# First transform of an SSM's response: data stationary against a moving constant, or the constant stationary against moving data

## The chip, the core and the metric

The kernel runs on one core of one Trainium2 chip. The metric is the device time of one execution in microseconds (us); less is better. A core has five engines that run side by side, each through its own instruction stream in order: TensorE (PE, with its weight loads shown apart as PEld), VectorE (DVE), ScalarE (ACT), GpSimd (POOL) and SyncE (SP). Matmuls write to PSUM, of which a tile of 128 x 512 floats is one bank; the other engines empty it. SP and POOL issue nearly all of this kernel's DMAs.

## The reference

The output is a sum of three parts over `x` of 2048 positions and 576 channels, normalised to `xn`:

```python
x = A_u
xn = _layernorm(x, axis=-1)
return x + _A_ref(xn, ...) + _B_ref(xn, B_w1, B_w2)

# _A_ref: a state space model as a long convolution, 128 complex states for each channel
P = jnp.exp(logdA[:, :, None] * l[None, None, :])
K = jnp.einsum("dn,dnl,dn->dl", Cc, P, dB).real          # response, 576 x 2048
...
y = irfft2(rfft2(xn padded) * rfft2(K padded)) + xn * Dskip
# _B_ref
out = silu(xn @ w1) @ w2                                   # 576 -> 4608 -> 576
```

## The kernel before

**Two streams.** The feed-forward part (`ffn()`, the "main" stream) is a chain of matmuls: `ph` (L298 to L300) makes 128 hidden rows for 512 positions, ScalarE and VectorE turn them into `gh` and `gl` (L306 to L308), and `po` (L328) multiplies these with `w2` and is added to `acc` by VectorE (L333). The convolution and all else are the "side" stream. A function `weave` interleaves the two by a table of fractions (`marks`), so that the side work is written in between. The order in which the instructions then stand on each engine is not that of the code: the framework's scheduler plays the program through with its own estimates of time and lets each engine take what is ready first, with `high_priority` and `issue_after` (`behind`) as hints. This order is fixed when the program is built. At run time each engine goes through its list, and an instruction that waits holds up all behind it on that engine.

**Rounded parts.** Matmuls of plain float32 show as two records each in the profile. The kernel therefore splits most operands into a rounded high part and the rest (`F32R`; names ending in h and l) and multiplies high x high, high x low and low x high, one fast record each. L298 and L328 are such; the two matmuls that the change touches, `kp` and `z`, were plain float32.

**The response.** `kgen` walks through 36 chunks of 16 channels. For a chunk VectorE and ScalarE make angles (`th`, L809, L811, L826), sines and cosines (L825 to L829), magnitudes (`mag`, in the tile `C`, L830 and L834) and from these two tables `S` and `C` (L845, L846). The magnitudes are products of powers: `powers` (L792 to L805), called for two chunks at a time, holds in `pw` the powers 0 to 7 of four bases per channel. It copies the bases in on ScalarE (L795) and makes the rest with three VectorE products (L800: square; L801: powers 3 and 4; L802: powers 5 to 7), and then `al` (L804). `S` and `C` have two buffers each.

After every second chunk, 18 times in all, TensorE contracts the tables over the 128 states into one PSUM bank `kp`: 64 matmuls of 32 x 64 (L866), K for 32 channels as 32 x 64 matrices of time. I call this event "a kp", and what lies between two of them "a stretch". ScalarE copies `kp` to `kt` (L873). Then comes the first transform `z` (L881), the subject of the change: for each of four column groups and two halves of the partitions, a 64 x 128 piece of `kt` is loaded as the stationary operand and the constant `f1` (64 x 128) moves. The two halves of the array work on different data at once (`tile_position` 0 and 64) and fill one PSUM bank each. ScalarE copies the two banks to `stage` (L889), and after every fourth chunk SP stores `stage` to `d1k` in DRAM (L894).

**The input's first transform.** `spread` is woven into `kgen`, one step per chunk from the third chunk on: `xn` is split (L149, L150), multiplied with the constant `s1` (L154, L155; `s1` holds both rounded parts of the same 128 x 128 constant, 128 stationary columns), copied to `u1` (L156) and stored by POOL to `d1u` (L157). `u1` has one buffer.

**After the response** the second half of the hidden layer goes on by Winograd's scheme, whose operands (`s1l`, `s2l`, ...) VectorE and ScalarE prepare in `wino_x` (L596 to L635) as soon as `kgen` is written; then `spectral` reads `d1u` and `d1k` back and does the second transforms, and `conv` the last. PSUM's pool `pss` has three banks, which `kp`, the two `z`, and `spread`'s `pu` share.

Of the kernel before, what the change touches and what calls it, by code (L numbers as in the profile page):

```python
# [10 lines left out]
F32 = mybir.dt.float32  # L11
# [30 lines left out]
def kernel(  # L42
# [14 lines left out]
    cs1: bass.AP,  # L57
    cf1: bass.AP,
    cm23: bass.AP,
# [28 lines left out]
    ident = cst.tile([P, P], F32, name="ident")  # L88
    f1 = cst.tile([P, P], F32, name="f1")
    s4 = None  # L90
# [47 lines left out]
    def spread(up):  # L138

        s1 = up.tile([P, 2, P], F32R, name="s1", bufs=1)  # L140
        nc.gpsimd.dma_start(s1, cs1)
        for j in range(NJ):
            src = up.tile([P, D], F32, tag="xr", name="xr")
            nc.sync.dma_start(src, dxn[:, j])
            for m in range(2):
                lo, hi = slice(64 * m, 64 * m + 64), slice(64 - 64 * m, 128 - 64 * m)
                u1 = up.tile([P, D], F32, tag="u1", name="u1")
                sp = up.tile([P, D], F32R, tag="sp", name="sp")
                nc.scalar.copy(sp[lo, :], src[lo, :])  # L149
                nc.vector.tensor_sub(sp[hi, :], src[lo, :], sp[lo, :])  # L150
                for h in range(2):
                    hs = slice(h * HD, (h + 1) * HD)
                    pu = pss.tile([P, 512], F32, tag="pss", name="pu")
                    nc.tensor.matmul(pu[:, :HD], s1[:, 0, :], sp[:, hs], start=True, stop=False)  # L154
                    nc.tensor.matmul(pu[:, :HD], s1[:, 1, :], sp[:, hs], start=False, stop=True)  # L155
                    nc.scalar.copy(u1[:, hs], pu[:, :HD])  # L156
                nc.gpsimd.dma_start(  # L157
                    d1u.rearrange("(p m j) d -> m j p d", m=2, j=NJ)[m, j], u1)
                yield j
# [477 lines left out]

    kl = yp = pa = kfp = w1x = tail_at = None
    kf = {}

    def natural(nat):
# [47 lines left out]
        r = nat.tile([P, 4 * D], F32, tag="r", name="r")  # L689
        for k, lag in enumerate((256.0, 64.0, 8.0, 1.0)):  # L690
            nc.scalar.activation(ex.rearrange("n (d k) -> n k d", k=4)[:, k, :], lrT, AF.Tanh, scale=0.5 * lag)
# [65 lines left out]

    def kgen():
        fT, rhoT, phiT = (kf[n] for n in ("f", "rho", "phi"))
        with tc.tile_pool(name="kg", bufs=1) as kg, tc.tile_pool(name="stg", bufs=1) as stg:  # L760
# [31 lines left out]
            def powers(i):  # L792
# [7 lines left out]
                nc.vector.tensor_mul(pv[:, :, 2], pv[:, :, 1], pv[:, :, 1])  # L800
                nc.vector.tensor_mul(pv[:, :, 3:5], pv[:, :, 1:3], pv[:, :, 2:3].broadcast_to([P, R, 2]))  # L801
                nc.vector.tensor_mul(pv[:, :, 5:8], pv[:, :, 1:4], pv[:, :, 4:5].broadcast_to([P, R, 3]))  # L802
                for q in range(2):
                    nc.vector.tensor_mul(split(al[:, q]), split(pw[:, q, :, 1, 0:4]), col(rhoT, i + q, 4))  # L804
                return al  # L805
# [12 lines left out]
            for i in range(NCK):  # L818
# [16 lines left out]
                    mag[:, :, 32:96].rearrange("n d (x y) -> n d x y", y=8),  # L835
                    pk[:, :, 2, :].unsqueeze(3).broadcast_to([P, W, 8, 8]),
                    pk[:, :, 3, :].unsqueeze(2).broadcast_to([P, W, 8, 8]))
                if i + 1 < NCK:
# [16 lines left out]
                for e in (1, 0):  # L855
                    S, C = tabs[e]
                    for gl in range(2):
                        for gp_ in range(2):
                            o = e * 256 + (gl * 2 + gp_) * 64
                            for q in range(4):  # L860
                                ch = gp_ * CH + gl * 4 + q
                                dst = kp[32 * q:32 * q + 32, o:o + 64]
                                begins = e == 1 and gl == 0 and gp_ == 0
                                with tc.high_priority(), behind(None if begins else first):
                                    for n, t in enumerate((C, S)):
                                        mm = nc.tensor.matmul(dst, t[:, ch, :32], t[:, ch, 32:],  # L866
                                                              start=begins and n == 0, stop=True,
                                                              tile_position=(0, 32 * q), skip_group_check=True)
                                if begins:
                                    first = mm.ins  # L870
                tabs = []
                kt = kg.tile([P, 512], F32, tag="kt", name="kt")
                nc.scalar.copy(kt, kp)  # L873

                z = [pss.tile([P, 512], F32, tag="pss", name="z") for _ in range(2)]
                first = None
                for eg in range(4):
                    for h in (1, 0):
                        rows = slice(64 * h, 64 * h + 64)
                        with tc.high_priority(), behind(first):  # L880
                            mm = nc.tensor.matmul(z[h][:, eg * P:(eg + 1) * P], kt[rows, eg * P:(eg + 1) * P], f1[rows],  # L881
                                                  start=True, stop=True, tile_position=(64 * h, 0))
                        first = first or mm.ins
                r = (i - 1) % NRUN
                if r == 0:
                    stage = stg.tile([P, 64, NRUN * CH], F32, tag="stage", name="stage")
                sv = stage[:, :, r * CH:(r + 2) * CH].rearrange("p k (e h c) -> p h e k c", h=2, c=2)
                for h in range(2):
                    nc.scalar.copy(sv[:, h], z[h].rearrange("p (e k c) -> p e k c", e=4, c=2))  # L889
# [132 lines left out]
    def side():  # L1022
        nonlocal s4, kl, yp, pa, kfp, w1x, tail_at
        marks = (0.1357, 0.613, 0.855)
# [9 lines left out]
        with tc.tile_pool(name="kf", bufs=1) as kfp:  # L1034
            for n in ("f", "rho", "phi"):
                kf[n] = kfp.tile([P, D], F32, name=n + "T")
            with tc.tile_pool(name="nat", bufs=1) as nat, tc.tile_pool(name="pb", bufs=2) as pb:
                nt = natural(nat)
                tiles = iter(range(8, NJ, 2))
                for at, tables in ((0.0, 1), (0.02, 0), (0.035, 0), (gate_of(1), 1), (0.06, 0), (gate_of(2), 1), (0.08, 0), (0.085, 1)):  # L1040
# [7 lines left out]
            with behind(pins["sd"]):  # L1048
                nc.gpsimd.dma_start(f1, cf1)
            nc.sync.dma_start(vt, cv)  # L1050
            with tc.tile_pool(name="up", bufs=1) as up, tc.tile_pool(name="w1x", bufs=1) as w1x:
                sp = spread(up)
                for n, at in enumerate(kgen()):
                    if n > 1:
# [41 lines left out]
def _constants():  # L1096
# [4 lines left out]
    cs = np.stack([np.cos(th), np.sin(th)], 2)  # L1101
    s1 = np.zeros((2, 2, 32, 32, 2, 2), f8)
    f1 = np.zeros((2, 2, 32, 32, 2, 2), f8)
    for q in range(2):
        s1[:, q, :, :, :, q] = cs
        f1[:, q, :, :, :, q] = cs
    s4 = np.broadcast_to(cs.transpose(2, 1, 0) / L, (2, 2, 32, 32)).reshape(P, 32)
    s1 = np.stack(_hi_lo(s1.reshape(P, P)), 1)
    f1 = f1.reshape(P, P)
    n2 = np.arange(64)  # L1110
# [21 lines left out]
        "cs1": s1,  # L1132
        "cf1": f1,
        "cm23": m23,
# [27 lines left out]
```

## Time and profile before

| what | value |
|---|---|
| median of 3 runs | 1121.45 us (1119.86 to 1123.09) |
| the profiled execution | 1121.59 us, its span 1119.7 us |
| busy over the span: PE, DVE, ACT, POOL | 97%, 85%, 65%, 13% |
| granted TensorE clock | 1.0 throughout |
| the stage of the 18 kp | 170 to 658 us of the span |
| z (L881) | 288 records, that is 144 matmuls |
| stores to d1u | 32 of 288 KB from POOL |

The span is the time from the first to the last instruction that the profiler shows; the execution's own time has 1.9 us more around it. A row of a group of instructions gives its line, engine and operation, what it writes and reads, its shapes and count, then busy time and mean duration, then the idle time of its engine just before and what ended it. Matmuls overlap one another, so the duration of one record is longer than the step from one to the next, and the step is what counts; on VectorE and ScalarE too one instruction starts a little before the one ahead has ended.

### The profile page before, as it was taken

The numbers are of one execution on the slowest core, as the hardware profiler recorded it, in microseconds if no ns is written. First come the engines' busy times: TensorE is split into PE (matmuls) and PEld (weight loads), VectorE is DVE, ScalarE is ACT, GpSimd is POOL, SyncE is SP. The second block draws the span as 40 slices with busy tenths as digits, with TensorE's granted clock in tenths as the row PEclk, the third lists the DMA queues.
The fourth block names the chain that finished last, engine by engine and source line by source line (L and its number), as shares of the span: only waits on it lengthen the run. The fifth ranks groups of instructions, "written<-read, shape, count | busy, mean of one in ns | idle before, by whom it ended". The sixth has DMA issues, their size and how long they took to land.

```text
span 1119.7 us, 23109 instructions
## 1 busy us (share of the span) xinstructions
PE 1091.6 (97%) x9101; PEld 987.6 (88%) x9101; DVE 950.0 (85%) x1615; ACT 728.1 (65%) x1285; POOL 140.5 (13%) x244
## 2 busy tenths in 40 slices
PE   6998999999999999999999999999999999999998
PEld 5997989889988899898899988899989998999787
DVE  6698899999999999999999978988878888886333
ACT  4665455776777766676667645877767877785330
POOL 1022100000000000000330001112212112111220
PEclk9999999999999999999999999999999999999999
DMA  9455632436353536356964235456455565543985
GB/s 272 141 156 177 194 124 82 144 85 176 105 154 128 150 108 172 120 138 236 237 190 92 72 65 183 133 175 178 140 165 178 163 187 157 167 157 116 247 200 139
DMA packets 161870, 173.68 MB, mean 155 GB/s; under 512 B 88497, under 2 KB 127425, under 8 KB 161121
## 3 DMA queue, kind: packets, MB, share of 16 engines
q1 hardware_dynamic: 137200, 106.75, 34.5%
q0 software_dynamic: 23888, 63.67, 19.2%
q10 hardware_dynamic: 672, 1.77, 0.7%
q8 instruction: 72, 1.18, 0.4%
q14 instruction: 38, 0.30, 0.1%
HBM read 109.64 MB, written 62.60 MB: 154 GB/s over the span
## 4 chain that ended last, share of the span: by engine, by line
PE 70%; DVE 10%; DMA 9%; ACT 5%; issue 4%; SPq 1%; POOL 1%; ACTq 0%; DVEq 0%; POOLq 0%
PE po L328 30%; PE ph L298 16%; PE pb L453 5%; PE kp L866 3%; DMA w<-dw 2%; PE pc L453 2%; DMA w1r<-in_B_w_dram 2%; PE pb L994 2%; PE pu L994 2%; PE pk L994 2%; PE ph L299 1%; PE ph L300 1%; PE z L881 1%; PE pa L453 1%; DMA w2r<-in_B_w_dram 1%
## 5 line engine op out<-in xcount | busy, mean ns | idle before, releaser
L328 PE MATMUL po<-w,gh 128*128 128x288 f32 x2304 | 475.1, 297 | 6.2 <-ACT w L284 2.1
L328 PEld LDWEIGHTS po<-w,gh 128*128 128x128 f32 x2304 | 376.5, 188 | 22.1 <-DMA w<-dw 2.7
L328 PE MATMUL po<-w,gl 128*128 128x288 f32 x1152 | 334.9, 296 | 0.6 <-DVE gl L308 0.6
L328 PEld LDWEIGHTS po<-w,gl 128*128 128x128 f32 x1152 | 215.2, 188 | 2.6 <-DVE gl L308 0.9
L333 DVE TENSOR_TENSOR acc<-po,acc 128x288 f32<-128x288 f32 x296 | 130.3, 452 | 59.7 <-PE po L328 58.6
L298 PE MATMUL ph<-xh,w1h 128*128 128x512 f32 (+1 forms) x368 | 99.1, 388 | 0.9 <-ACT xh L123 0.7
L298 PE MATMUL ph<-xl,w1h 128*128 128x512 f32 (+1 forms) x368 | 98.5, 386 | 0.0
L298 PE MATMUL ph<-xh,w1l 128*128 128x512 f32 (+1 forms) x368 | 97.9, 383 | 0.0
L306 ACT ACTIVATE gf<-ph 128x512 f32<-128x512 f32 (+1 forms) x92 | 53.3, 579 | 60.4 <-PE ph L300 41.8
L298 PEld LDWEIGHTS ph<-xl,w1h 128*128 128x128 f32 x368 | 67.6, 191 | 12.8
L298 PEld LDWEIGHTS ph<-xh,w1l 128*128 128x128 f32 x368 | 66.6, 189 | 11.7
L298 PEld LDWEIGHTS ph<-xh,w1h 128*128 128x128 f32 x368 | 65.2, 191 | 11.2 <-ACT xh L123 1.0
L157 POOL DMA_DIRECT2D d1u<-u x32 | 17.5, 547 | 405.8 <-ACT u L156 404.5
L825 ACT ACTIVATE c<-th,magic 128x1040 f32<-128x1040 f32 x36 | 42.0, 1168 | 40.2 <-DVE C L846 28.0
L307 ACT CAST gh<-gf 128x512 fp32r<-128x512 f32 (+1 forms) x92 | 55.3, 602 | 15.5 <-PE po L328 14.5
L903 POOL DMA_DIRECT2D m<-in_cm_dram x64 | 33.9, 531 | 250.8 <-PE pu L994 147.1
L308 DVE TENSOR_TENSOR gl<-gf,gh 128x512 fp32r<-128x512 f32 (+1 forms) x92 | 60.7, 662 | 3.5 <-ACT gh L307 3.3
L827 ACT ACTIVATE c<-th 128x1040 f32<-128x1040 f32 x36 | 38.7, 1076 | 33.7 <-DVE th L826 33.6
L845 DVE TENSOR_TENSOR S<-th,C 128x1024 f32<-128x1024 f32 x36 | 44.0, 1222 | 12.1 <-ACT th L828 12.0
L470 DVE TENSOR_TENSOR gl<-gf,gh 128x512 fp32r<-128x512 f32 x56 | 38.0, 688 | 11.9 <-ACT gh L469 11.6
L370 ACT CAST w1h<-w1r 128x512 fp32r<-128x512 f32 (+2 forms) x56 | 34.6, 621 | 20.3 <-DMA w1r<-in_B_w_dram 14.6
L826 DVE SCALAR_TENSOR_TENSOR th<-c,th 128x1040 f32<-128x1040 f32 x36 | 44.5, 1237 | 0.7 <-ACT c L825 0.5
(271 smaller groups left out, 2384.5 us busy)
## 6 DMA issues: line engine op xcount, KB each, us to landing
w1r<-in_B_w_dram SPq DMA_DIRECT2D x35, 512.0 KB, 4.2
dw<-w SPq DMA_DIRECT2D x28, 576.0 KB, 4.5
w<-dw POOLq DMA_DIRECT2D x28, 576.0 KB, 6.6
w2r<-in_B_w_dram SPq DMA_DIRECT2D x44, 288.0 KB, 5.0
d1u<-u POOLq DMA_DIRECT2D x32, 288.0 KB, 2.7
d1k<-stage SPq DMA_DIRECT2D x18, 512.0 KB, 7.3
ur<-d1u SPq DMA_DIRECT2D x32, 288.0 KB, 3.3
kr<-d1k SPq DMA_DIRECT2D x32, 288.0 KB, 2.8
```

What stands on the lines that cost most here:

```text
L298: nc.tensor.matmul(ph, w[:, kt, :], v[:, kt, a:e], start=n + kt == 0, stop=False)
L306: nc.scalar.activation(gf, ph, AF.Silu)
L307: pins["gh"] = nc.scalar.copy(gh, gf).ins
L308: pins["gl"] = nc.vector.tensor_sub(gl, gf, gh).ins
L328: pins["pe"] = nc.tensor.matmul(po[:, :HD], gs[g][:, js], ws[:, w, hs], start=n == 0 and j not in begun, stop=n == 3 * len(terms) - 1, ski ...
L333: nc.vector.tensor_add(acc[j][:, hs], po[:, :HD], acc[j][:, hs])
L453: pins["pe"] = nc.tensor.matmul(dst, a[:, kt], v[:, kt], start=start and n == 0, stop=stop and n == 5, skip_group_check=True).ins
L825: nc.scalar.activation(c65, th, AF.Identity, bias=magic)
L826: nc.vector.scalar_tensor_tensor(th, c65, MAGIC, th, op0=ALU.subtract, op1=ALU.subtract)
L827: nc.scalar.activation(c65, th, AF.Abs)
L845: nc.vector.tensor_mul(ov3, t[:, :, 0:64].rearrange("n d (x y) -> n d x y", y=32), mv3)
L994: nc.tensor.matmul(dst, st, mv[:, hs], start=n == 0, stop=n == 3 * len(terms) - 1)
```

## The change

Four things change, all in `kgen`, `spread` and the constants.

- `z` is turned round. The constant is stationary (`s1`, both rounded parts, which `spread` uses too), and the data move, 512 columns at a time: `kp` is split into `kh` (ScalarE, in place of the copy `kt`) and `kl` (a new VectorE subtraction that reads PSUM), and for each half of the partitions there are three matmuls: high x high, low part of the constant x high, high part of the constant x `kl`. Six matmuls of 512 columns replace eight of 128 in plain float32. `kl` takes the buffer of `u1`, so that the two exclude each other.
- One constant serves both transforms. The constant `f1` and its tile go; the columns of `s1` are put in the order (q, k, c). For `spread` the rows of `u1` come out in that order, so its store is two DMAs of 64 partitions each. For `kgen` the channels in `kp` are placed differently, and the result has k over the partitions; the copy to `stage` now reads PSUM with a step of 64 floats, and the store to `d1k` sends 64 neighbouring rows from each partition. Each element of that store is still 32 floats long.
- Powers 2 and 4 are made by ScalarE (`Square`, on 128 and 96 elements per partition) behind its copy of the bases; VectorE keeps power 3 (128 elements) and powers 5 to 7 (288 elements in place of 384). The base that needs no powers above 3 moves to the last place.
- `s1` is loaded ahead of `kgen`.

```diff
     def spread(up):
 
-        s1 = up.tile([P, 2, P], F32R, name="s1", bufs=1)
-        nc.gpsimd.dma_start(s1, cs1)
+        du = d1u.rearrange("(k q m j) d -> m j q k d", q=2, m=2, j=NJ)
...
-                nc.gpsimd.dma_start(
-                    d1u.rearrange("(p m j) d -> m j p d", m=2, j=NJ)[m, j], u1)
+                for q in range(2):
+                    nc.gpsimd.dma_start(du[m, j, q], u1[64 * q:64 * q + 64])
...
-                pv = pw.rearrange("n r d k e -> n (r d k) e")
-                R = 2 * W * 4
-                nc.vector.tensor_mul(pv[:, :, 2], pv[:, :, 1], pv[:, :, 1])
-                nc.vector.tensor_mul(pv[:, :, 3:5], pv[:, :, 1:3], pv[:, :, 2:3].broadcast_to([P, R, 2]))
-                nc.vector.tensor_mul(pv[:, :, 5:8], pv[:, :, 1:4], pv[:, :, 4:5].broadcast_to([P, R, 3]))
+                pv = pw.rearrange("n r d k e -> n (r d) k e")
+                nc.scalar.activation(pv[:, :, :, 2], pv[:, :, :, 1], AF.Square)
+                nc.scalar.activation(pv[:, :, 0:3, 4], pv[:, :, 0:3, 2], AF.Square)
+                nc.vector.tensor_mul(pv[:, :, :, 3], pv[:, :, :, 1], pv[:, :, :, 2])
+                nc.vector.tensor_mul(pv[:, :, 0:3, 5:8], pv[:, :, 0:3, 1:4],
+                                     pv[:, :, 0:3, 4:5].broadcast_to([P, 2 * W, 3, 3]))
...
-                kt = kg.tile([P, 512], F32, tag="kt", name="kt")
-                nc.scalar.copy(kt, kp)
+                kh = kg.tile([P, 512], F32R, tag="kh", name="kh")
+                kl = up.tile([P, D], F32R, tag="u1", name="kl")[:, :512]
+                nc.scalar.copy(kh, kp)
+                nc.vector.tensor_sub(kl, kp, kh)
 
                 z = [pss.tile([P, 512], F32, tag="pss", name="z") for _ in range(2)]
                 first = None
-                for eg in range(4):
+                for n, (k, v) in enumerate(((0, kh), (1, kh), (0, kl))):
                     for h in (1, 0):
                         rows = slice(64 * h, 64 * h + 64)
                         with tc.high_priority(), behind(first):
-                            mm = nc.tensor.matmul(z[h][:, eg * P:(eg + 1) * P], kt[rows, eg * P:(eg + 1) * P], f1[rows],
-                                                  start=True, stop=True, tile_position=(64 * h, 0))
+                            mm = nc.tensor.matmul(z[h], s1[rows, k], v[rows], start=n == 0, stop=n == 2,
+                                                  tile_position=(64 * h, 0))
...
-                sv = stage[:, :, r * CH:(r + 2) * CH].rearrange("p k (e h c) -> p h e k c", h=2, c=2)
+                sv = stage[:, :, r * CH:(r + 2) * CH].rearrange("p n (e h c) -> p h e n c", h=2, c=4)
                 for h in range(2):
-                    nc.scalar.copy(sv[:, h], z[h].rearrange("p (e k c) -> p e k c", e=4, c=2))
+                    nc.scalar.copy(sv[:, h], z[h].rearrange("p (e c n) -> p e n c", e=2, c=4))
...
-                    kv = d1k.rearrange("(k n) (g d) -> g n k d", n=64, g=2)
+                    kv = d1k.rearrange("(k n) (g d) -> g k n d", n=64, g=2)
```

Since the scheduler plans the whole program anew, the order of all engines differs from the first kp on, also in instructions that the diff does not touch. The lines of the changed program are up to 3 lower than those before at the same place (L328 becomes L325, L298 L295). Three places show it.

TensorE behind the tenth kp, before: the eight matmuls of `z` stand in one block, ahead of `spread`'s `pu`.

```order
L328 MATMUL po<-w_4706,gh 128x288 x2
L328 MATMUL po<-w_4706,gl 128x288 x2
L328 MATMUL po<-w_4504,gh 128x288
L881 MATMUL z<-f_69,kt 128x128 x8
L154 MATMUL pu<-sp,s_2126 128x288
L155 MATMUL pu<-sp,s_2126 128x288
```

The same place now:

```order
L325 MATMUL po<-w_5274,gh 128x288 x2
L325 MATMUL po<-w_5274,gl 128x288
L880 MATMUL z<-kh,s_1388 128x512 x4
L325 MATMUL po<-w_5425,gh 128x288 x2
L880 MATMUL z<-kl,s_1388 128x512 x2
L151 MATMUL pu<-sp,s_1388 128x288
L152 MATMUL pu<-sp,s_1388 128x288
```

The four matmuls that need `kh` alone and the two that need `kl` are parted by others; so it is behind each of the 18 kp.

VectorE behind the tenth kp, before: the products of powers, spread among the tables.

```order
L800 TENSOR_TENSOR pw<-pw 128x128
L333 TENSOR_TENSOR acc_247<-po,acc_247 128x288
L845 TENSOR_TENSOR S<-th,C 128x16x2x32
L846 SCALAR_TENSOR_TENSOR S<-th,C 128x16x32
L801 TENSOR_TENSOR pw<-pw 128x128x2
L150 TENSOR_TENSOR sp<-xr,sp 64x576
L845 TENSOR_TENSOR C<-c_5309,C 128x16x2x32
L846 SCALAR_TENSOR_TENSOR C<-c_5309,C 128x16x32
L809 TENSOR_TENSOR th<-vt,fT 128x1040
L802 TENSOR_TENSOR pw<-pw 128x128x3
```

The same place now (L843 and L844 are the tables, L283 and L305 the rests `w2` and `gl` of the main stream):

```order
L872 TENSOR_TENSOR kl<-kp,kh 128x512
L330 TENSOR_TENSOR acc_293<-po,acc_293 128x288
L305 TENSOR_TENSOR gl<-gf,gh 128x512
L283 TENSOR_TENSOR w_5425<-w2r,w_5425 128x576
L305 TENSOR_TENSOR gl<-gf,gh 128x512
L843 TENSOR_TENSOR C<-c_5336,C 128x16x2x32
L283 TENSOR_TENSOR w_5431<-w2r,w_5431 128x576
L798 TENSOR_TENSOR pw<-pw 128x128
L844 SCALAR_TENSOR_TENSOR C<-c_5336,C 128x16x32
L807 TENSOR_TENSOR th<-vt,fT 128x1040
```

`kl` has come in and one product of powers is gone; and the main stream's `gl` and `w2` splits now crowd into this stretch, ahead of the tables that the eleventh kp waits for.

ScalarE behind the tenth kp, now:

```order
L792 COPY pw<-eb 128x128
L303 ACTIVATE gf<-ph 128x512
L796 ACTIVATE pw<-pw 128x128
L888 COPY stage<-z 128x2x64x4 x2
L304 CAST gh<-gf 128x512
L153 COPY u_4860<-pu 128x288
L797 ACTIVATE pw<-pw 128x32x3
```

Before, the copy of the bases stood there with no square behind it. The second square now stands behind the copies of `z` and `pu`, which wait for TensorE.

More of the change, by code (lines that the diff above doesn't have):

```diff
@@ L57 @@
     cs1: bass.AP,
-    cf1: bass.AP,
     cm23: bass.AP,
@@ L689, in natural @@
         r = nat.tile([P, 4 * D], F32, tag="r", name="r")
-        for k, lag in enumerate((256.0, 64.0, 8.0, 1.0)):
+        for k, lag in enumerate((256.0, 8.0, 1.0, 64.0)):
             nc.scalar.activation(ex.rearrange("n (d k) -> n k d", k=4)[:, k, :], lrT, AF.Tanh, scale=0.5 * lag)
@@ L856, in kgen @@
                     S, C = tabs[e]
[L857 to L870, printed above, removed]
+                    for c4 in range(4):
+                        o = e * 256 + c4 * 64
+                        for q in range(4):
+                            ch = q % 2 * CH + q // 2 * 4 + c4
+                            dst = kp[32 * q:32 * q + 32, o:o + 64]
+                            begins = e == 1 and c4 == 0
+                            with tc.high_priority(), behind(None if begins else first):
+                                for n, t in enumerate((C, S)):
+                                    mm = nc.tensor.matmul(dst, t[:, ch, :32], t[:, ch, 32:],
+                                                          start=begins and n == 0, stop=True,
+                                                          tile_position=(0, 32 * q), skip_group_check=True)
+                            if begins:
+                                first = mm.ins
@@ L1047, in side @@
                             phase0(pb, (j, j + 1))
-            with behind(pins["sd"]):
-                nc.gpsimd.dma_start(f1, cf1)
             nc.sync.dma_start(vt, cv)
             with tc.tile_pool(name="up", bufs=1) as up, tc.tile_pool(name="w1x", bufs=1) as w1x:
+                s1 = up.tile([P, 2, P], F32R, name="s1", bufs=1)
+                with behind(pins["sd"]):
+                    nc.gpsimd.dma_start(s1, cs1)
                 sp = spread(up)
-                for n, at in enumerate(kgen()):
+                for n, at in enumerate(kgen(up)):
                     if n > 1:
```

21 lines of the change are left out of this document (8 added, 13 removed).

## The prediction

> **What bounds the kernel now.** I read the page's shares of busy time first (the table ahead has them: TensorE leads), then the busy times by stretch, then the waits, then the timeline around one z.
>
> ```profile
> 170.00:651.00 481.00, 479.55 (x4980) 432.50 (x4979) 459.28 (x676) 330.25 (x492) 37.36 (x72) 1.00 0.50 139
> 650.00:700.00 50.00, 48.34 (x410) 42.69 (x409) 39.39 (x62) 26.77 (x48) 6.23 (x11) 1.00 0.52 138
> ```
>
> These are the stage of the kp and the 50 us behind it (columns: stretch, length, then busy PE, PEld, DVE, ACT, POOL). In the stage TensorE has no gap to speak of, but VectorE is busy for 459.3 of 481 us too: 95%. What each waits for there:
>
> ```profile
> PE po L328 <- DVE acc L333: 0.6, 1, 0.6
> PE po L328 <- ACT gh L307: 0.5, 1, 0.5
> ...
> DVE C L830 <- PE kp L866: 5.7, 7, 1.4
> ```
>
> TensorE waits 1.1 us in 481 (total, times, longest), so its work sets the pace, and VectorE follows by little. VectorE cannot run far ahead: with two buffers of `C` it waits for the kp that still reads one (L830). How far ahead it is shows in the end of the last table of a pair (its start and duration, VectorE's timeline) against the start of the kp that reads it (chain of waits, which is a few hundredths late):
>
> ```profile
> 473.83 0.68 DVE L846 SCALAR_TENSOR_TENSOR C<-c,C 128x512 f32<-128x512 f32 x1
> ```
>
> ```profile
> 476.52 1.99 PE kp L866 x124
> ```
>
> and, two kp later,
>
> ```profile
> 506.98 0.68 DVE L846 SCALAR_TENSOR_TENSOR C<-c,C 128x512 f32<-128x512 f32 x1
> ```
>
> ```profile
> 512.18 2.00 PE kp L866 x125
> ```
>
> These are the smallest lead of the 18, 2 us, and the largest, 4.5; I use 3.1.
>
> **The change part by part.** *z on TensorE.* Its timeline, in three cuts:
>
> ```profile
> 480.81 0.29 PE L328 MATMUL po<-w,gl 128*128 128x288 f32 x1
> 481.04 0.49 PE L881 MATMUL z<-f,kt 64*128 64x128 f32 x4
> 481.04 0.60 PE L881 MATMUL z<-f,kt 64*128 64x128 f32 x6
> 481.04 1.16 PE L881 MATMUL z<-f,kt 64*128 64x128 f32 x16
> 482.13 0.40 PE L154 MATMUL pu<-sp,s 128*128 128x288 f32 x1
> ```
>
> and a later place where halves of the array work side by side:
>
> ```profile
> 1044.80 0.39 PE L453 MATMUL pb<-s2h,w1l 128*128 128x512 f32 x1
> 1045.12 0.69 PE L1013 MATMUL py<-ys,s 64*32 64x288 f32 x8
> 1045.74 0.50 PE L453 MATMUL pb<-s2h,w1l 128*128 128x512 f32 x1
> ```
>
> ```profile
> 441.76 2.72 PE ph L298 x12
> 472.42 4.11 PE po L328 x31
> ```
>
> From the chain (last fence), a 512-column matmul of rounded parts steps 2.72/12 = 0.227 us and a 288-column one 4.11/31 = 0.133. The step into z is 481.04 - 480.81 = 0.23, 0.10 more than a po; from z's start to the next matmul it is 1.09. So z costs 1.19. Two more records lengthen it by 0.11 (0.49 to 0.60): the two halves run together, eight pairs make 0.88, and 0.31 is for going in, filling and coming out. At the py matmuls two steps of four records take 0.62, of which 2 x 0.11 x 288/128 = 0.50 is columns, and the way in 0.32 - 0.23 = 0.09: 0.21 for one block of long matmuls. The new z has three pairs of 512 columns in two blocks: 3 x 0.227 + 2 x 0.21 = 1.10, which I round up for the trace's step of 0.01 to 1.12. That is 0.07 less than 1.19, times 18: **-1.3 us**. Bounds: 0.31 for each block gives 1.30 and +2.0; 0.19 (way in and out only) gives 1.06 and -2.3. Split in two by `kl`, the change pays for its shorter z nearly all that it gains.
>
> That the halves overlap was shown for plain float32, which takes a column at half the rate. [...]
>
> *VectorE's work.* Its prices are the mean durations less the overlap with the next instruction:
>
> ```profile
> L333 DVE TENSOR_TENSOR acc<-po,acc 128x288 f32<-128x288 f32 x127 | 55.0, 452 | 3.2 <-PE po L328 2.9
> L308 DVE TENSOR_TENSOR gl<-gf,gh 128x512 fp32r<-128x512 f32 x64 | 43.8, 686 | 0.1
> L826 DVE SCALAR_TENSOR_TENSOR th<-c,th 128x1040 f32<-128x1040 f32 x34 | 42.1, 1237 | 0.6 <-ACT c L825 0.5
> L845 DVE TENSOR_TENSOR S<-th,C 128x1024 f32<-128x1024 f32 x34 | 41.5, 1222 | 11.2 <-ACT th L828 11.1
> L268 DVE TENSOR_TENSOR w1l<-w1r,w1h 128x640 fp32r<-128x640 f32 x32 | 25.2, 817 | 0.0
> L286 DVE TENSOR_TENSOR w<-w2r,w 128x576 fp32r<-128x576 f32 x32 | 24.1, 752 | 0.0
> L150 DVE TENSOR_TENSOR sp<-xr,sp 64x576 fp32r<-64x576 f32 x31 | 23.3, 753 | 1.0
> L801 DVE TENSOR_TENSOR pw<-pw 128x256 f32<-128x256 f32 x16 | 10.0, 626 | 0.1
> L802 DVE TENSOR_TENSOR pw<-pw 128x384 f32<-128x384 f32 x16 | 8.9, 555 | 0.1
> L800 DVE TENSOR_TENSOR pw<-pw 128x128 f32<-128x128 f32 x16 | 6.9, 432 | 0.0
> L804 DVE TENSOR_TENSOR al<-pw,rhoT 128x64 f32<-128x64 f32 x32 | 5.7, 221 | 0.0
> ```
>
> ```profile
> 663.45 0.37 DVE acc L333
> 663.82 0.60 DVE gl L308
> ```
>
> The chain shows 0.37 for an acc of 452 ns and 0.60 for a gl of 686: 0.085 us overlap. Out go L800 (0.35), L801 (0.54) and L802 (0.47), 1.36 in all. In come power 3 like L800 (0.35), powers 5 to 7 at 288/384 of L802's columns (0.37) and `kl`, 512 columns like a gl (0.60): 1.32. VectorE's total stays the same, so what its instructions wait for, and in which stretch they stand, decides. All else of two chunks' tables (two each of L809, L826 and L834, four L845: ten of about 1.14; eight of 512 columns at 0.60; al twice 0.14) is 16.5, so 17.8 with the new powers and `kl`.
>
> *Waits at the kp.* The order tells how the scheduler filled each stretch. Counted by these prices from kp to kp (TensorE) and from last table to last table (VectorE), before the change VectorE has more than TensorE by at most 0.6 us in any stretch, so its lead never runs out. After it, 15 of the 17 stretches have VectorE equal or below. Between the tenth and eleventh kp TensorE has 47 po, 8 pu and 44 of 512 columns: 55 x 0.133 + 44 x 0.227, with kp (2.1) and z (1.1) and 0.3 for joints 20.8 us. VectorE has 17.8 + 3 sp (0.785 with its idle time), 3 L286, 4 gl and 3 acc = 25.7. In the next it is 23.1 against 21.3, in the one after (71 po, 42 long; 4 L268, 2 sp, 1 L286, 3 gl, 7 acc) 23.5 against 27.4. A lead of 3.1 - 4.9 leaves a wait of 1.8 at the eleventh kp, then 1.8 of lead, then 1.8 - 3.9: 2.1 at the thirteenth. That is 3.9 us. VectorE also waits 11.1 + 0.5 us for ScalarE (the idle times of L845 and L826) over 17 stretches, 0.7 each, which no lead absorbs here: then 2.5 + 3.5 = 6.0. I take **+5.0**, with 0 (the lead absorbs all) and 8 as bounds. Behind a kp that waits stands all of TensorE's list, so this is on the path.
>
> *The end of the response.* Before, VectorE had the last kp's stretch in hand and then prepared Winograd's operands without a pause:
>
> ```profile
> 651.03 2.00 PE kp L866 x123
> ```
>
> ```profile
> 669.67 0.73 PE L453 MATMUL pc<-s1l,w1h 128*128 128x512 f32 x2 [0.51 <-DVE s1l L602]
> ```
>
> ```profile
> PE po L328 <- DVE acc L333: 1.1, 1, 1.1
> ```
>
> TensorE came to `s1l` 669.67 - 0.51 - 651.03 = 18.1 us after the kp and waited 0.5; the last row is its other wait in these 50 us. In the new order it has 14.2 us of work to the first `s1h`, 15.0 to `s1l` with joints; VectorE must do `kl` (3.3 us after the kp's start: kp, `kh`, `kl`) and 14.4 more: 17.7. A wait of 2.7 in place of the 0.5 and the 1.1: **+1.0**, bounds -1 and +3.
>
> *What is hidden.* ScalarE's squares:
>
> ```profile
> L889 ACT COPY stage<-z 128x512 f32<-128x512 f32 x36 | 21.5, 654 | 2.2 <-PE z L881 2.0
> L795 ACT COPY pw<-eb 128x128 f32<-128x128 f32 x17 | 7.6, 446 | 3.5 <-DVE C L834 3.5
> ```
>
> Two per pair at L795's 0.45 are 16 us, on an engine busy for 330 of 481: covered by its 31% idle time, and where VectorE is late, up to 0.9 us a pair of it shows. The copy to `stage` now reads PSUM with a step of 64; I keep 654 ns, since nothing waits for it but `pss`. [...]
>
> `u1`'s store in two DMAs adds 32 issues on POOL, which has 93% of its time free. `kl` waits for both to land:
>
> ```profile
> L157 POOL DMA_DIRECT2D d1u<-u x32 | 17.5, 547 | 405.8 <-ACT u L156 404.5
> ```
>
> ```profile
> DMA to landing us min/median/max: 2.4/2.7/5.5
> ```
>
> With 0.55 for the second issue that is 3.3 us after the copy (the second row is of these stores). At nearly all of the 18 places far more work stands in the order between the store and `kl`; behind the twelfth kp VectorE has 2.4 us between, and behind the thirteenth the two stand near each other too, so there it may stop for about 1 us each: inside the 5.0. POOL's stores behind `out` and `acc` transfers come at the same places as before. `d1k`'s runs keep their size; 0.
>
> The sum, on the profiled execution's 1121.6 (0.1 above the median): -1.3 + 5.0 + 1.0 = **1126**.
>
> **The rivals.** *No wait forms:* TensorE's stretches are light since the scheduler holds them longer, and the lead is 4.5 as at 507, VectorE's list being freer elsewhere. For it: 15 stretches of 17. Then -1.3 and half the end: 1121. *Faster:* the second block's way in and out falls together with the weight load, so that switching is paid once; z costs 0.68 + 0.21 = 0.89, 18 x 0.30 = 5.4 less, and no wait: 1116. It decides from a z under 1.0 (18 x 0.19 = 3.4) with no waits; against it, kp and z both show way in and way out at each place. [...] *They do not overlap:* six steps of 0.227 and 0.42 make 1.78, +0.59 x 18 = 10.6, and the waits shrink to 2 as TensorE gets slower: 1135. Against it: PSUM banks and partitions are apart, as in float32. *`kl` blocks VectorE:* it stands ahead of tables and waits for kp, `kh` and stores; at 0.5 us of each of 18 beyond my 5.0 it is +9: 1133. It decides from 0.2 us each.
>
> **How the numbers follow.** Chances: forecast 0.43 (own range 1121.5 to 1130), no wait 0.26, faster 0.10, overlap in part 0.06, no overlap 0.08, `kl` blocks 0.07. A measurement of this kernel can tell 0.3%, 3.4 us: below 1118.1 is faster, above 1124.8 slower. Slower: 0.62 of the forecast case (0.27) and all of the last three (0.21): 0.48. Faster: 0.10, and a third of no wait: 0.19. Same: 0.33. The range 1115 to 1136 leaves out a part of the faster case, down to 1112, and of the last two.
>
> **What the profile after would show.** z in blocks of 4 and 2, with steps of about 0.23 for two records, and a sum of 1.1 per kp; at 1.8 the halves do not overlap. Waits of TensorE at kp for VectorE's tables near the eleventh and thirteenth kp, 1.5 to 3.5 us each; none elsewhere. `pc<-s1l` waiting 2 to 3 us. ACT busy 16 us more in the stage, VectorE's busy time equal. I would be wrong if TensorE waits for `kl` at z itself, or if stretches before the tenth kp already wait.

## The result and the profile after

The changed kernel takes 1140.22 us (median of 4 runs, 1135.53 to 1140.62), the kernel before 1120.86: a ratio of 1.0167, 95% interval 1.0146 to 1.0188. It is slower, and by more than the predicted range (to 1136) holds. The profiled execution is the fastest of the four, 1135.53 us with a span of 1133.8; the comparison below is of the two profiled spans, 14.1 us apart.

| where it went | before | after | difference |
|---|---|---|---|
| z on TensorE, 18 times | 1.19 each | 1.27 each | +1.4 |
| TensorE's named waits, whole span | 23.8 | 29.0 | +5.2 |
| lost to a lower TensorE clock, while TensorE had work | 0.0 | 5.1 | +5.1 |
| not named (rest of the 14.1) | | | 2.4 |

The second row is the sum of the waits view, the third the sum of one minus the granted clock over windows of 1 us. Of the second, +7.3 us come in the stage of the kp and +3.9 behind it, up to 730 us; ahead of the stage and behind 730 us the changed kernel waits 6.0 us less. The 4.7 us between the profiled execution and the median have no trace. The stage of the kp, and the end of the response, by windows (columns as in the prediction):

```profile
170.00:651.00 481.00, 472.32 (x4613) 413.36 (x4612) 444.48 (x654) 332.31 (x513) 52.51 (x102) 1.00 0.50 138
650.00:730.00 80.00, 72.83 (x517) 63.06 (x516) 63.70 (x104) 40.45 (x72) 8.89 (x16) 0.96 0.42 112
```

TensorE and VectorE both do less in the same 481 us: over the stage neither engine became the bound, both waited. In the second row the granted clock is 0.96; in the kernel before it is 1.00 in every window of the span. TensorE's waits of the changed kernel from 430 to 500 us, where the kernel before had none:

```profile
PE z L880 <- DVE kl L872: 2.3, 2, 1.3
PE po L325 <- ACT gh L304: 1.6, 1, 1.6
PE po L325 <- DVE w L283: 1.4, 1, 1.4
PE po L325 <- ACT w L281: 1.3, 1, 1.3
PE z L880 <- ACT kh L871: 0.9, 1, 0.9
PE po L325 <- DVE acc L330: 0.8, 1, 0.8
```

and from 650 to 730 us, 7.1 us in all (before: 3.2):

```profile
PE po L325 <- DVE acc L330: 2.0, 1, 2.0
PE pb L993 <- ACT w1h L367: 1.9, 1, 1.9
PE po L325 <- ACT gf L465: 1.7, 1, 1.7
PE pb L993 <- ACT kb L922: 0.9, 1, 0.9
PE pa L450 <- ACT pa L511: 0.6, 1, 0.6
```

No row is a kp that waits for tables. The first group begins with weights. SP's queue, then ScalarE, which rounds the weights, then TensorE:

```profile
451.47 4.52 SPq L893 DMA_DIRECT2D d1k<-stage  x2
456.09 3.59 SPq L285 DMA_DIRECT2D dw<-w  x1
459.73 0.42 SPq L272 DMA_DIRECT2D w2r<-in_B_w_dram  x1
```

```profile
464.44 0.66 ACT L281 CAST w<-w2r 128x576 fp32r<-128x576 f32 x1
```

```profile
465.14 0.66 PE L325 MATMUL po<-w,gh 128*128 128x288 f32 x3 [1.34 <-ACT w L281]
467.20 0.61 PE L325 MATMUL po<-w,gh 128*128 128x288 f32 x1 [1.40 <-DVE w L283]
```

The load of `w2r` is issued at 459.73, behind 8 us of SP's issuing, and lands after some 4.5 us (the median of these loads), at about 464.2: an estimate. ScalarE comes to it at 464.44, straight from sines and cosines of the tables. Both were late at the same time, and TensorE waited for the rounded part and for VectorE's rest. The chain of waits tells more. From 460.1 to 481.4 us it holds neither a DMA nor a matmul; it runs over ScalarE and VectorE alone. Four of its pieces (start, duration):

```profile
463.51 1.23 DVE S L843
465.26 1.22 DVE C L843
466.48 0.67 DVE w L283
478.61 0.68 DVE kl L872
```

So the rest `w` was late because it stood behind the tables on VectorE (ScalarE's part had been ready since 465.1), and `kl`, behind the eleventh kp, likewise. Two waits of 1.3 and 1.4 us follow each other, and then, by windows of 2 us:

```profile
464.00:466.00 2.00, 0.66 (x3) 0.43 (x3) 2.00 (x3) 1.69 (x4) 0.02 (x1) 1.00 0.97 380
466.00:468.00 2.00, 0.80 (x3) 0.80 (x4) 2.00 (x4) 0.16 (x1) 1.03 (x2) 0.74 0.44 97
468.00:470.00 2.00, 2.00 (x45) 1.72 (x47) 2.00 (x4) 1.01 (x1) 0.00 (x0) 0.50 0.97 286
470.00:472.00 2.00, 2.00 (x102) 1.91 (x93) 2.00 (x4) 0.22 (x1) 0.00 (x0) 0.91 0.64 220
```

The clock falls to 0.50 for some 3.4 us and costs 1.7. The same happens after the 2.0 us wait at 680 and after 1.94 and 0.90 at 720: three times 1.7. The other runs of the changed kernel have mean clocks of 0.992 to 0.994, against the profiled 0.995, which is 1 to 3 of the 4 to 5 us by which they are longer. One z of the changed kernel, from its timeline:

```profile
325.97 0.29 PE L325 MATMUL po<-w,gl 128*128 128x288 f32 x1
326.19 0.73 PE L880 MATMUL z<-kh,s 64*128 64x512 f32 x4
326.85 0.53 PE L325 MATMUL po<-w,gh 128*128 128x288 f32 x2
...
330.62 0.39 PE L297 MATMUL ph<-x,w1l 128*128 128x512 f32 x1
330.93 0.49 PE L880 MATMUL z<-kl,s 64*128 64x512 f32 x2
331.36 0.40 PE L151 MATMUL pu<-sp,s 128*128 128x288 f32 x1
```

From the start of a block to the next matmul 0.66 and 0.43, and the way in costs 0.22 - 0.13 and 0.31 - 0.23, together 1.26. The rows are rounded to 0.01; 1.27 is used here.

### The profile page after: what moved, and what is told of

The parts are those of the page before. It is cut to its first block, busy times and chain, and to the rows that moved or that the text cites. A ratio compares the mean times of both kernels' runs of the same rounds, so it can differ in the third digit from the quotient of the medians.

```text
span 1133.8 us, 22859 instructions
## 1 busy us (share of the span) xinstructions
PE 1100.5 (97%) x8921; PEld 981.9 (87%) x8921; DVE 951.2 (84%) x1615; ACT 738.0 (65%) x1321; POOL 155.7 (14%) x275
## 3 DMA queue, kind: packets, MB, share of 16 engines
q8 instruction: 70, 1.15, 0.4%
## 4 chain that ended last, share of the span: by engine, by line
PE 85%; DMA 4%; DVE 4%; ACT 3%; issue 2%; POOL 0%; SPq 0%; DVEq 0%; ACTq 0%; POOLq 0%
PE po L325 36%; PE ph L295 20%; PE pb L450 6%; PE pc L450 3%; PE kp L863 3%; PE pb L993 2%; PE pu L993 2%; PE pk L993 2%; PE ph L297 2%; PE ph L296 2%; PE z L880 1%; PE pa L450 1%; DMA w1r<-in_B_w_dram 1%; PE pc L456 1%; PE pu L151 1%
## 5 line engine op out<-in xcount | busy, mean ns | idle before, releaser
L325 PE MATMUL po<-w,gh 128*128 128x288 f32 x2304 | 478.9, 298 | 9.4 <-DVE acc L330 2.8
L325 PEld LDWEIGHTS po<-w,gh 128*128 128x128 f32 x2304 | 376.9, 188 | 31.6 <-issue 7.0
L325 PE MATMUL po<-w,gl 128*128 128x288 f32 x1152 | 334.8, 296 | 0.5 <-DVE gl L305 0.5
L325 PEld LDWEIGHTS po<-w,gl 128*128 128x128 f32 x1152 | 216.1, 189 | 3.2 <-DVE gl L305 0.8
L295 PE MATMUL ph<-xh,w1h 128*128 128x512 f32 (+1 forms) x368 | 99.5, 388 | 1.1 <-ACT xh L121 0.7
L295 PE MATMUL ph<-xl,w1h 128*128 128x512 f32 (+1 forms) x368 | 99.0, 385 | 0.0
L295 PE MATMUL ph<-xh,w1l 128*128 128x512 f32 (+1 forms) x368 | 98.4, 383 | 0.0
L155 POOL DMA_DIRECT2D d1u<-u x64 | 33.6, 531 | 430.8 <-ACT u L153 430.5
L295 PEld LDWEIGHTS ph<-xl,w1h 128*128 128x128 f32 x368 | 66.9, 190 | 13.2 <-issue 0.7
L295 PEld LDWEIGHTS ph<-xh,w1l 128*128 128x128 f32 x368 | 66.1, 188 | 12.3 <-issue 0.4
L295 PEld LDWEIGHTS ph<-xh,w1h 128*128 128x128 f32 x368 | 65.2, 191 | 11.7 <-ACT xh L121 1.0
L305 DVE TENSOR_TENSOR gl<-gf,gh 128x512 fp32r<-128x512 f32 (+1 forms) x92 | 60.5, 660 | 3.0 <-ACT gh L304 2.8
L843 DVE TENSOR_TENSOR S<-th,C 128x1024 f32<-128x1024 f32 x36 | 43.9, 1220 | 18.6 <-ACT th L826 18.6
L807 DVE TENSOR_TENSOR th<-vt,fT 128x1040 f32<-128x1040 f32 x36 | 44.4, 1235 | 0.1
```

The source lines that it names most:

```text
L295: nc.tensor.matmul(ph, w[:, kt, :], v[:, kt, a:e], start=n + kt == 0, stop=False)
L305: pins["gl"] = nc.vector.tensor_sub(gl, gf, gh).ins
L325: pins["pe"] = nc.tensor.matmul(po[:, :HD], gs[g][:, js], ws[:, w, hs], start=n == 0 and j not in begun, stop=n == 3 * len(terms) - 1, ski ...
L807: nc.vector.tensor_mul(split(th), row(vt[:, 0:65], 65), col(fT, i, 65))
L843: nc.vector.tensor_mul(ov3, t[:, :, 0:64].rearrange("n d (x y) -> n d x y", y=32), mv3)
```

## The experiments

Two theories stood against each other. W: the change's own work makes the time (z, `kl`, squares, by engine). O: the work matters little; the scheduler's new order leaves waits somewhere, and some of the longer ones halve the clock.

**Undoing parts.** The powers back on VectorE, in the changed kernel:

```diff
-nc.scalar.activation(pv[:, :, :, 2], pv[:, :, :, 1], AF.Square)
-nc.scalar.activation(pv[:, :, 0:3, 4], pv[:, :, 0:3, 2], AF.Square)
+nc.vector.tensor_mul(...)      # the three products of before
```

> The changed kernel with all powers on VectorE again (three products, bases in the old order); the turned transform, the one constant and the two stores stay. Theory W (the work itself sets the time, and ScalarE's squares make its results late): the waits of TensorE between 464 and 490 us go, z stays at 1.27 us a kp, 1125 us (1121 to 1130). Theory O (any new order leaves a few waits of one to two us somewhere, and those near 2 us halve TensorE's clock for some 3.4 us): the waits are not tied to the squares; they stand at other places, and the time may be anything from 1120 to 1140, with waits over 1 us and half-clock stretches together explaining it.

1128.32 us, ratio 1.0066 (1.0047 to 1.0085): 12 less than the changed kernel. No wait from 430 to 500; waits of 6.8 us remain from 650 to 730, and the granted clock there is 0.94, which is 4.8 us lost, about three stretches of half clock. Without the squares the first group of waits is gone; but the order is another too, and a run below has the squares and not these waits. Alone, in the kernel before (the same edit the other way round), the squares cost nothing:

> The kernel before with the powers as in the change alone (two squares on ScalarE, bases reordered); z, constants and stores as before. Theory W with the squares at fault: 1127 to 1135, TensorE waiting for ScalarE's gh or w in the kp stage. Theory W with z and kl at fault: VectorE is relieved by 0.64 us a pair, 1119 to 1122. Theory O: 1118 to 1135, whatever it is explained by waits over 1 us and by half clock, at places that differ from the changed kernel's.

1121.02 us, ratio 1.0019 (0.9998 to 1.0039), although VectorE's busy time falls by 10 us. So 10 us less of VectorE's busy time do not make this kernel faster, and ScalarE's squares do not make it slower. Whether they do so together with the rest of the change, or the order alone does, these two runs do not tell.

**One block of z.** `kl`'s pair first, so that the others follow it:

```diff
-for n, (k, v) in enumerate(((0, kh), (1, kh), (0, kl))):
+for n, (k, v) in enumerate(((0, kl), (0, kh), (1, kh))):
```

> The changed kernel with kl's two matmuls ahead of kh's four, so that all six of a z stand in one block. By the traces a block costs 0.29 us beside its columns (0.09 in, 0.10 after the first pair, 0.10 out), whatever its length: z falls from 1.27 to 0.97 us. Theory W: 18 x 0.30 = 5.4 us less than the changed kernel, 1130 to 1135. Theory O: z at 0.97 all the same, but the time is set by the waits of the new order, 1115 to 1140.

1133.8 us, ratio 1.0102 (1.0076 to 1.0129), 6.4 less. Its z:

```profile
307.53 0.43 PE L325 MATMUL po<-w,gh 128*128 128x288 f32 x2
307.89 0.50 PE L880 MATMUL z<-kl,s 64*128 64x512 f32 x2
308.23 0.63 PE L880 MATMUL z<-kh,s 64*128 64x512 f32 x4
308.79 0.40 PE L151 MATMUL pu<-sp,s 128*128 128x288 f32 x1
```

0.90 from start to next and 0.09 in, 0.99: near the expected 0.97. That the total fell by about 18 x 0.28 = 5.0 looks like theory W; the runs below show that it is not to be read so.

**The price of a block.** Blocks of half-array pairs among full matmuls; nothing of the reference is computed.

> No part of the reference is computed: trains of 512-column matmuls of rounded parts at full rate, broken by blocks of 1, 2, 3, 4 and 6 pairs of half-array matmuls, and by pauses of TensorE of about 1 to 3.5 us while VectorE works. Block price constant: n pairs cost 0.227 n + 0.29 us. Price by pair: n x 0.33. [...]

```profile
36.79 0.40 PE L89 MATMUL z<-v,s 64*128 64x512 f32 x2
37.12 2.13 PE L83 MATMUL b<-v,s 128*128 128x512 f32 x8
39.18 1.66 PE L89 MATMUL z<-v,s 64*128 64x512 f32 x12
40.77 1.43 PE L83 MATMUL b<-v,s 128*128 128x512 f32 x5
```

The last block, six pairs, takes 1.59 to the next matmul; blocks of 1, 2, 3 and 4 took 0.42, 0.66, 0.90 and 1.12. That is 0.19 + 0.233 a pair, and 0.09 for the way in: 0.28 for each block at all of these lengths, and halves that overlap (0.233 a pair, against 0.227 for one full matmul). The pauses did not come about here, since the matmuls behind them were put ahead; a second kernel made them.

**What halves the clock.** The next train of 64 matmuls moves what VectorE makes in the pause:

> No part of the reference is computed: trains of 512-column matmuls of rounded parts at full rate with pauses of TensorE between them, of about 1.5 to 4 us, while VectorE makes the next train's operand; then three pairs of shorter pauses with 4, 8 and 16 matmuls between, and four short ones. If one pause of about 2 us is what halves the clock: pauses up to 1.7 us leave the clock at 1.0, and each of 2 us or more is followed by some 3.4 us at 0.5. [...]

Trains after pauses (start, duration, in brackets the pause); 14.82 us is a train at full clock:

```profile
103.43 14.80 PE L82 MATMUL b<-g,s 128*128 128x512 f32 x64 [1.67 <-DVE g L95]
120.03 16.43 PE L82 MATMUL b<-g,s 128*128 128x512 f32 x64 [1.80 <-DVE g L95]
138.39 14.82 PE L82 MATMUL b<-g,s 128*128 128x512 f32 x64 [1.94 <-DVE g L95]
155.28 14.82 PE L82 MATMUL b<-g,s 128*128 128x512 f32 x64 [2.07 <-DVE g L95]
172.70 17.70 PE L82 MATMUL b<-g,s 128*128 128x512 f32 x64 [2.60 <-DVE g L95]
235.12 14.82 PE L82 MATMUL b<-g,s 128*128 128x512 f32 x64 [3.52 <-DVE g L95]
254.19 16.30 PE L82 MATMUL b<-g,s 128*128 128x512 f32 x64 [4.25 <-DVE g L95]
272.03 1.19 PE L82 MATMUL b<-g,s 128*128 128x512 f32 x4 [1.53 <-DVE g L95]
274.75 16.27 PE L82 MATMUL b<-g,s 128*128 128x512 f32 x64 [1.54 <-DVE g L95]
```

Length alone did not decide: a pause of 1.80 us halved the clock, those of 1.94, 2.07 and 3.52 did not; the five single pauses of 1.21 to 1.67 did not, but two of 1.53 and 1.54 with four matmuls between did, as two of 1.34 and 1.40 with three between at 464 us in the changed kernel (with 8 and 16 between, two of 1.53 to 1.54 did not). By windows of 1 us each halving took 1.71 or 3.42 us of clock, that is 0.50 for 3.4 us or for 6.8, and the train behind the pause was 1.5 to 2.9 us longer. These rows contradict the expected rule: single pauses of 2.07 and 3.52 left the clock at 1.0, and two of 1.53 and 1.54 halved it. What decides beside the length they do not show.

**SP's queue.** The stores of `stage` from POOL:

```diff
-nc.sync.dma_start(kv[gp_, :, :, ...], stage[...])
+nc.gpsimd.dma_start(kv[gp_, :, :, ...], stage[...])
```

> The changed kernel with the stores of stage to d1k issued by POOL in place of SP; all else is left to the scheduler. In the changed kernel SP takes 4.5 us to issue two of these, 3.6 for the next store, and then issues the weights that TensorE waits for at 464. If SP's queue is what makes them late: no wait for weights or their parts near 464, 3 to 6 us less than the changed kernel, 1130 to 1136. If VectorE's lateness behind the tenth kp makes it: the waits between 464 and 490 us stay (5 us or more), 1136 to 1142.

1130.71 us, ratio 1.0096 (1.0068 to 1.0125). The waits for weights are gone (430 to 500: 1.9 us in all), and the time is 9.5 less, where 3 to 6 less and 1130 to 1136 had been expected. But its order differs too, and the next runs show that this alone can do it. So this run does not show that SP's queue was the cause; in the changed kernel's trace ScalarE came to the weights no earlier than they landed.

**z turned round without parts.** Whole `kt`, plain float32, one pair of 512 columns; everything else of the change left out:

```diff
-for eg in range(4):                       # eight of 128 columns
-    nc.tensor.matmul(z[h][:, eg * P:(eg + 1) * P], kt[rows, eg * P:(eg + 1) * P], f1[rows], ...)
+nc.tensor.matmul(z[h], f1[rows], kt[rows], ..., tile_position=(64 * h, 0))
```

> The kernel before with z turned round alone, in plain float32: kt whole, the constant f1 in the new column order, one pair of 512-column matmuls (two records each) for a kp; no kl, the powers, s1 and the stores to d1u as before. By the block price of 0.29 and 0.227 for a pair of records, z takes 0.29 + 2 x 0.227 = 0.74 us in place of 1.19: 18 x 0.45 = 8 us less on TensorE. Theory W: TensorE's bound gives 1112 to 1115. VectorE as the next bound (459 of 481 us busy): part of the gain is lost in waits for tables, 1115 to 1120. Theory O: 1113 to 1130, by where the new order waits.

> As the kernel with z turned in plain float32, and two of the powers on ScalarE as in the change: VectorE has 0.64 us less for each of the 18 pairs, 11.5 us. Theory W: no waits for tables, 1110 to 1114. Theory O: 1112 to 1130, with waits over 1 us at other places than in the kernel without the squares.

1121.79 and 1122.26 us, ratios 1.0001 (0.9985 to 1.0018) and 1.0012 (0.9998 to 1.0027). The expectation of z was wrong:

```profile
289.85 0.29 PE L328 MATMUL po<-w,gl 128*128 128x288 f32 x1
290.07 1.13 PE L879 MATMUL z<-kt,f 64*128 64x512 f32 x4
291.13 0.40 PE L154 MATMUL pu<-sp,s 128*128 128x288 f32 x1
```

It takes 1.06 and 0.09 in, 1.15. Less the 0.19 of a block, each of the two records of a plain float32 matmul takes (1.06 - 0.19) / 2 = 0.43 for 512 columns, about twice the 0.227 of rounded parts, so turning round without parts changes next to nothing (1.15 against 1.19). What counts more: the other placement in `kp`, the strided copy to `stage`, the new store to `d1k` and the squares together cost nothing here that these runs can tell.

**The same work in another order.** One number of the table of marks, which says where in the main stream the response ends or begins:

```diff
-marks = (0.1357, 0.613, 0.855)
+marks = (0.1357, 0.611, 0.855)
```

> The kernel before with one number changed, the end of the response's span in the table of marks (0.613 becomes 0.611): the same instructions in another order. Theory O: an order's waits are luck, and the kernel before stands at a lucky one: 1122 to 1132, with waits and half clock at other places. Theory W: the same work, 1119 to 1123.

> As the kernel with 0.611, but with 0.615. Theory O: 1122 to 1132. Theory W: 1119 to 1123.

> The kernel before with the first number of its table of marks changed, 0.1357 becomes 0.1377 (the response begins 0.55 steps later); 0.613 stays. If the kernel before stands at a place that was found by search in both numbers: 1126 to 1135, as with 0.611 and 0.615. If 0.613 alone is the tuned number: 1118 to 1123.

The kernel before takes 1133.45 with 0.611, 1130.53 with 0.615 (ratios 1.0123 and 1.0099, intervals 1.0105 to 1.0141 and 1.0080 to 1.0118) and 1119.12 with 0.1377 in place of 0.1357 (0.9987, 0.9975 to 1.0000). With 0.611 there is a wait at the same place as the changed kernel's second group, 650 to 730 us,

```profile
PE po L328 <- ACT gh L469: 4.1, 1, 4.1
```

and four stretches of half clock, 8.5 us lost over a span that is 11.3 us longer; the named waits are 25.4 us over the span, only 1.6 more than before. Not an instruction was added on any of PE, VectorE, ScalarE and GpSimd. The changed kernel with the same numbers:

> The changed kernel with the same number changed from 0.613 to 0.611. Theory O: the waits at 464 to 490 and 680 to 723 are those of one order; another has others, and the time is anywhere from 1122 to 1140. Theory W (the change's work itself makes the waits): 1136 to 1143, with the waits behind a kp again.

> The changed kernel with 0.615 in place of 0.613; its order differs from the changed kernel's less than the one with 0.611 does. Theory O: anywhere from 1122 to 1140. Theory W: 1136 to 1143.

1132.57 and 1139.04. With 0.611 the waits from 430 to 500 are one of 0.5 us; with 0.615, whose order differs little from the changed kernel's, they stand at 464 to 488 again and at the same instructions.

**Both together.** Powers on VectorE and z in one block, at three numbers, z in one block with the squares, and the squares alone, at 0.611:

> The changed kernel with all powers on VectorE again and the six matmuls of z in one block. The kernel with the powers back alone took 1128.3; z falls from 1.27 to 0.97, 5.4 us. If the price of z adds to whatever the order's waits are: 1123 (1119 to 1126). If each new order draws its waits anew: 1118 to 1136, and the sum of waits and half clock tells which.

> The changed kernel with z in one block and 0.611 in the table of marks. The changed kernel with 0.611 alone took 1132.6. If the price of z adds: 1127 (1123 to 1130). If the waits are drawn anew: 1118 to 1138.

> Powers on VectorE, z in one block, and 0.611. If 0.611 costs what it cost the kernel before (13 us over its 0.613): about 1136 by the run with 0.613 at 1123. If it costs nothing of its own, the same as that run; below 1117 it would beat both kernels.

> Powers on VectorE, z in one block, and 0.615 in the table of marks. By the runs with 0.613 (1131.2) and 0.611 (1128.8): 1125 to 1135. Below 1117 it would beat both kernels.

> The kernel before with the two squares on ScalarE and 0.611 in the table of marks; with 0.613 it took 1121.0. If the mark of 0.613 is what the kernel before is tuned to, this loses as the kernel before did at 0.611: 1130 to 1136. If the kernel before was merely unlucky at 0.611: 1119 to 1125.

The kernel before, run beside each of these, took 1118.9 to 1120.9.

| kernel | 0.611 | 0.613 | 0.615 |
|---|---|---|---|
| before | 1133.5 | 1120.9 | 1130.5 |
| before, squares on ScalarE | 1129.1 | 1121.0 | |
| before, z turned in plain float32 | | 1121.8 | |
| changed | 1132.6 | 1140.2 | 1139.0 |
| changed, powers on VectorE | | 1128.3 | |
| changed, z in one block | 1131.7 | 1133.8 | |
| changed, both | 1128.8 | 1131.2 | 1129.9 |

z in one block saves 5 us of TensorE's work in each of its kernels, and the time goes by -6.4, -0.9 and +2.9 against the same kernel with two blocks (the last pair's ratios to the kernel before, 1.0093 to 1.0135 against 1.0047 to 1.0085, do not overlap). TensorE's named waits grow in all three pairs, by 6.2, 4.9 and 4.9 us: what z gives up comes back as waits. That fits waits drawn anew with each order; an engine other than TensorE that sets the pace there would look the same. VectorE's total cannot be that alone: with the powers back VectorE is busy 10 us longer (961 against 951), and three kernels with them back are 3 to 12 us faster than the same without. No version with the change beats the kernel before.

What the table shows: the kernel before and the four near it (squares, z turned in plain float32 with and without squares, another first number) take 1119 to 1122 at 0.613, and the two of them that were tried at 0.611 or 0.615 lose 8 to 13 us there. With `kl` and the one constant, ten kernels at all three numbers take 1128 to 1140. At the same number the changed kernel is 19 us slower than the kernel before at 0.613, 8.5 slower at 0.615 and 1 faster at 0.611. So what the change costs depends on the order, and an order alone can cost nearly as much; that the change's work costs nothing of its own is not shown. What stays open: which of these parts (`kl` on VectorE, the buffer that it shares with `u1`, two stores to `d1u`, the earlier `s1`) takes the kernel out of the good place at 0.613, and why that number is good.

## Why the prediction was right or wrong

The sign was right (slower, at a chance of 0.48), the time was not: +5 was forecast, +19 came, outside the range. Of the profiled 14.1 us the sum had 4.7. The other 9.4 are z (2.7 more than forecast), the clock (5.1, forecast at nothing) and the 2.4 without a name, less 0.8 for the waits. That the waits over the whole span come out so near (+5.2 where 5.0 + 1.0 were forecast) is luck: in the two places that the prediction named they are 11.2, and 6.0 went away in places that it did not look at.

- **The clock: put at nothing.** The granted clock of before is 1.0, and the sum priced a wait at its length, without a reason given. Three waits or pairs of waits cost 1.7 us more each, 5.1 in all: the largest single error in the profiled span.
- **z: the term was mis-sized.** 0.21 for a block was read from the py matmuls; a block costs 0.28 to 0.29 (way in, first pair, way out), which the 0.31 of before's own z had shown. 1.27 in place of 1.12, +1.4 in place of -1.3. The upper bound (1.30, +2.0) held it, and the halves overlap: a pair steps 0.233, where a full matmul steps 0.227 and two apart 0.454. So the rival without overlap fell, and no run shows the overlap in part that stands at 0.06 in the chances.
- **Waits at the kp: the step failed.** No kp waited for tables. Counting VectorE's work from kp to kp named the right place and the right engine: the chain of waits runs over VectorE's tables there, with ScalarE's sines and cosines between. What was wrong is where the wait lands and how long it is. The order lets TensorE wait for what stands behind the tables, `w`, `kl` and `acc` on VectorE and `gh` on ScalarE, 2.7 us ahead of the eleventh kp and 5.6 behind it; 8.3 in all against 5.0. And the step took the stretch as a property of the change, while the changed kernel with 0.611 has the same work and 0.5 us there.
- **The end of the response: mis-sized.** +1.0 was forecast, at `pc`; it is 7.1 - 3.2 = +3.9, at `acc` (which stands behind Winograd's operands on VectorE), `gf`, `w1h`; `s1l` kept nobody waiting. Here too VectorE was late and the wait came at another instruction.
- **Hidden work: right in the main.** The squares' rows sum to 15.5 us (16 were forecast) and ScalarE's busy time grows by 9.9 over the span; VectorE's is equal (951.2 to 950.0), and the kernel before with the squares alone is no slower. The copy to `stage` with a step of 64 floats is no slower than the plain one (mean before 654 ns):

```profile
L888 ACT COPY stage<-z 128x512 f32<-128x512 f32 x36 | 19.3, 587 | 14.4 <-PE z L880 14.2
```

  which is 67 ns less a copy.
- **`kl` blocks VectorE: small.** VectorE waited at it once, 2.2 us, for `kh`. TensorE waited for `kl` at z twice, 2.3 us in all, which the prediction had named as a sign of being wrong.
- **What no term held:** that the kernel before sits at a setting from which another number alone takes 10 to 13 us. The rivals were all ways in which the change's work could cost; none was that a new order costs by itself.

## What to carry to other kernels

Where a scheduler orders the whole program and a table was tuned around it, compare a change with the old kernel in a few other orders too (one number of the table moved a little): here that alone took 10 to 13 us, more than any part of the change's work. In the changed kernel, whose TensorE is 97% busy, a wait of 1.99 us and two pairs close together (1.34 and 1.40, 1.94 and 0.90) cost 1.7 us more each by the clock; in the kernel of pauses 1.80 cost 1.6, and 1.94 and 2.07 cost nothing: price such a wait as a chance. And matmuls on half the array paid 0.28 us for each block of them, of one pair or of six, so keep their pairs together.

## What the hardware showed beyond that

- In the kernel of pauses a pause of 1.80 us halved the clock and one of 3.52 did not. What decides beside the length was not settled.
- Plain float32 cost 3.8 times the rounded parts' time for a column (two records of about 0.43 us for 512 columns, against one of 0.227), so three products of rounded parts (three pairs of 0.233) beat one plain matmul by little, 0.70 to 0.87, and here the price of the second block, 0.28, took more than that.
